# Loading q, k and v six chunks ahead instead of four in a fused attention and MLP kernel

## The chip, the cores and the metric

The kernel runs on one core of a Trainium2 chip. The metric is the device time of one execution in microseconds (us). The time of a kernel is a median over several executions on one chip, with the lowest and highest beside it; a point in time or a wait inside the kernel comes from one profiled execution. TensorE is PE in the profile, VectorE is DVE, ScalarE is ACT, GpSimd is POOL and SyncE is SP.

## The reference

```python
def _attn_ref(q, k, v):                      # q, k, v: 8 x 8 x 576 x 64, float32
    scores = scale * np.matmul(q, k.transpose(0, 1, 3, 2))
    Dmat = np.where(rel >= 0, gamma[:, None, None] ** rel[None], 0.0)   # decay by distance
    return np.matmul(scores * Dmat[None], v)

def _moe_ref(x, w_in, w_out):                # x: 4608 x 512; d_ff 2048
    h = x @ w_in
    g = h * np.clip(h + 3.0, 0.0, 6.0) / 6.0
    return g @ w_out
# reference: the attention's output, 4608 tokens of 512, goes through the MLP
```

## The kernel before

The attention works in chunks of 128 rows of one batch, all eight heads at once, with a running state between chunks. A batch of 576 rows gives four such chunks and one of 64 rows. There are 40 chunks, counted from 0; numbers 4, 9, 14 and so on are the small ones. Each chunk is loaded as float32, cast to half precision on GpSimd, transposed, and multiplied on TensorE. The MLP follows block by block, its matmuls woven between the chunks' work.

The load of a chunk takes a staging buffer and puts DMAs into the queue of SP: three of 256 KB for a full chunk, six of 64 KB for a small one.

```python
def load(b, c):
    t  = work.tile([P, 2, H, D] ..., FP32, tag="stgqk", bufs=5)
    tv = work.tile([P, H, D] ...,    FP32, tag="stgv",  bufs=5)
    for dst, src in ((t[:, 0], k), (t[:, 1], q), (tv, v)):
        if c < NCH:
            nc.sync.dma_start(dst, src[b, :, P*c:P*c + P, :]...)          # L86
            continue
        for x in range(2):
            nc.sync.dma_start(dst[x*REM:x*REM + REM], src[b, ...]...)     # L92
```

Steps carry the number of their chunk; the first after the opening is step 4. The step of chunk i does chunk i's work on TensorE, casts chunk i + 2, sends its transpose into the same queue, and loads a later chunk. The opening has loaded the first ones.

```python
def step(i):
    ...                                   # inter, update, keep, score, mix
    stage(cast, i + 2)                    # GpSimd
    if i + 2 > NCH + NPE - 1:
        stage(xpose, i + 2)               # nc.sync.dma_start_transpose, L124
    stage(load, i + 4)                    # L488
# ... in the opening:
    stage(load, NCH)
    for i in range(NCH + 1, NCH + 4):     # NCH = 4
        stage(load, i)
```

The second matmul of the MLP ends in a copy on ScalarE to a buffer of the pool `osb`, and the output DMA goes into SP's queue as well.

```python
def down(kb, mc, part):
    ...                                   # matmuls into pout, L526
    if part == 3:
        osb = work.tile([P, 2, DM], FP32, tag="osb", bufs=3)
        nc.scalar.copy(osb[:, 0], pout)                                    # L531
        nc.sync.dma_start(out[tok0 + P*mc:tok0 + P*mc + P, :], osb[:, 0])  # L533
```

## Time and profile before

| | kernel before |
|---|---|
| time, median (lowest to highest) of 4 runs | 315.67 us (314.45 to 322.81) |
| span of the profiled run, granted clock | 314.4 us, 0.995 |
| TensorE busy | 296.8 us, 94% |
| ScalarE's wait for an output DMA (fourth copy to `osb`) | 2.00 us, ends at 52.30 us |
| TensorE's waits for transposes near 96 and 102 us | 1.59 + 1.92 us |

How to read it: TensorE is the bound over most of the span, so a change of the loads can only matter in the short stretches in which TensorE stands still, and in what such a stretch does to the clock afterwards. For a DMA queue each timeline row is the start, the time that SP spent issuing, the line, and "out<-in". SP's rows stand in program order, so a row also shows what stood behind what. For an engine, the bracket at the end of a row is the idle time before it and what ended that. The prediction below shows these rows of the kernel before.

### The profile page before, as it was taken

How to read it: one execution, taken by the hardware profiler on the slowest of the kernel's cores; microseconds unless marked ns; L12 is line 12 of the kernel's file. 1: busy time of each engine (PE TensorE's matmuls, PEld its weight loads, DVE VectorE, ACT ScalarE, POOL GpSimd, SP SyncE). 2: the span in 40 equal slices, each digit the busy share in tenths (PEclk: the TensorE clock that was granted, in tenths of full speed). 3: DMA queues.
4: the chain of work that ended last, by engine and by line, in shares of the span. 5: the costliest groups of instructions: out<-in, count | busy, mean ns of one | idle time of the engine just before them, and what ended most of it. 6: DMA issues, size and time to landing. Idle time of an engine off the chain costs nothing.

```text
span 314.4 us, 6863 instructions
## 1 busy us (share of the span) xinstructions
PE 296.8 (94%) x2644; PEld 190.6 (61%) x2644; DVE 233.4 (74%) x435; ACT 162.4 (52%) x307; POOL 127.0 (40%) x154
## 2 busy tenths in 40 slices
PE   7899989989995998999999999999989999999994
PEld 2454447667542467656864686468646865684583
DVE  6797348475766599799778977897779778856781
ACT  7667235446435461476257624753566357526721
POOL 2780167462855479144073607231844070000000
PEclk9999999999999799999999999999999999999999
DMA  7999998739879969965259865980799252003003
GB/s 249 219 207 197 196 224 220 199 90 217 165 177 220 255 143 201 247 150 126 60 144 291 163 144 141 262 185 19 179 255 248 56 178 9 2 0 135 1 0 133
DMA packets 143264, 49.59 MB, mean 158 GB/s; under 512 B 134272, under 2 KB 140416, under 8 KB 143232
## 3 DMA queue, kind: packets, MB, share of 16 engines
q1 hardware_dynamic: 139008, 44.97, 62.0%
q0 software_dynamic: 4224, 4.19, 8.0%
q8 instruction: 20, 0.33, 0.4%
q14 instruction: 12, 0.10, 0.1%
HBM read 36.70 MB, written 9.44 MB: 147 GB/s over the span
## 4 chain that ended last, share of the span: by engine, by line
PE 64%; DMA 18%; POOL 6%; DVE 4%; ACT 3%; issue 2%; SPq 2%; POOLq 0%; DVEq 0%; ACTq 0%
PE ph L509 28%; PE accy L582 14%; DMA wout_160<-in_moe_w_out_dram 7%; PE accz L582 7%; PE pout L526 4%; PE accx L582 3%; DMA stgk_72<-in_k_dram 2%; PE po L354 2%; DMA qkt_4_3592<-natqk_4_3587 2%; ACT u L513 2%; DMA qkt_0_1558<-natqk_0_1553 2%; DMA out_dram<-osb 1%; DMA stgv_0_1791<-in_v_dram 1%; PE pu L274 1%; DMA stgqk_1_1498<-in_k_dram 1%
## 5 line engine op out<-in xcount | busy, mean ns | idle before, releaser
L513 ACT ACTIVATE u<-ph,cb 128x512 f32<-128x512 f32 x144 | 98.8, 689 | 36.0 <-PE ph L509 33.9
L509 PEld LDWEIGHTS <-win_159 128*128 128x128 f16 x704 | 62.1, 98 | 60.2 <-issue 2.8
L592 ACT COPY csum<-accy 128x256 f32<-128x256 f32 x42 | 15.7, 373 | 45.1 <-PE accy L582 45.1
L310 POOL TENSOR_TENSOR sd<-state_152,gp 128x512 f32<-128x512 f16 x7 | 7.3, 1040 | 39.2 <-DVE state_152 L305 26.2
L310 POOL TENSOR_TENSOR sd<-state_153,gp 128x512 f32<-128x512 f16 x7 | 7.3, 1041 | 25.7 <-DVE state_153 L305 16.5
L310 POOL TENSOR_TENSOR sd<-state_151,gp 128x512 f32<-128x512 f16 x7 | 7.3, 1040 | 24.0 <-DVE state_151 L305 16.8
L509 PE MATMUL ph<-xt_1198,win_159 128*128 128x512 f16 x64 | 16.1, 410 | 0.0
L526 PE MATMUL pout<-wout_160,gt_0_505 128*128 128x512 f16 x64 | 15.0, 379 | 0.9 <-DMA wout_160<-in_moe_w_out_dram 0.9
L514 DVE SCALAR_TENSOR_TENSOR gt_4_1565<-u,ph 128x512 f16<-128x512 f32 x16 | 10.7, 685 | 5.6 <-ACT u L513 5.6
L509 PE MATMUL ph<-xt_342,win_159 128*128 128x512 f16 x64 | 14.0, 379 | 0.7 <-ACT xt_342 L387 0.7
L509 PE MATMUL ph<-xt_2035,win_159 128*128 128x512 f16 x64 | 14.5, 380 | 0.0
L509 PE MATMUL ph<-xt_3027,win_159 128*128 128x512 f16 x64 | 14.5, 380 | 0.0
L509 PE MATMUL ph<-xt_3585,win_159 128*128 128x512 f16 x64 | 14.3, 379 | 0.0
L509 PE MATMUL ph<-xt_1617,win_159 128*128 128x512 f16 x64 | 14.3, 379 | 0.0
L509 PE MATMUL ph<-xt_2592,win_159 128*128 128x512 f16 x64 | 14.3, 379 | 0.0
L509 PE MATMUL ph<-xt_4018,win_159 128*128 128x512 f16 x64 | 14.0, 379 | 0.0
L514 DVE SCALAR_TENSOR_TENSOR gt_10_4472<-u,ph 128x512 f16<-128x512 f32 x16 | 11.0, 687 | 3.8 <-ACT u L513 3.8
L601 DVE TENSOR_TENSOR osb<-accz,csum 128x256 f32<-128x256 f32 x14 | 5.9, 423 | 10.5 <-PE accz L582 10.4
L608 DVE TENSOR_TENSOR osb<-accz,csum 128x256 f32<-128x256 f32 x14 | 5.8, 422 | 10.5 <-ACT csum L592 10.5
L514 DVE SCALAR_TENSOR_TENSOR gt_0_505<-u,ph 128x512 f16<-128x512 f32 x16 | 11.0, 687 | 2.6 <-ACT u L513 2.5
L514 DVE SCALAR_TENSOR_TENSOR gt_9_4109<-u,ph 128x512 f16<-128x512 f32 x16 | 10.8, 686 | 2.6 <-ACT u L513 2.4
L514 DVE SCALAR_TENSOR_TENSOR gt_8_3599<-u,ph 128x512 f16<-128x512 f32 x16 | 10.5, 683 | 2.8 <-ACT u L513 2.6
(736 smaller groups left out, 685.9 us busy)
## 6 DMA issues: line engine op xcount, KB each, us to landing
out_dram<-osb SPq DMA_DIRECT2D x14, 512.0 KB, 4.2
win_159<-in_moe_w_in_dram POOLq DMA_DIRECT2D x4, 512.0 KB, 9.5
wout_160<-in_moe_w_out_dram POOLq DMA_DIRECT2D x4, 512.0 KB, 18.3
out_dram<-osb SPq DMA_DIRECT2D x8, 256.0 KB, 3.6
stgq_66<-in_q_dram SPq DMA_DIRECT2D x1, 512.0 KB, 3.8
stgk_68<-in_k_dram SPq DMA_DIRECT2D x1, 512.0 KB, 4.6
stgq_70<-in_q_dram SPq DMA_DIRECT2D x1, 512.0 KB, 6.2
stgk_72<-in_k_dram SPq DMA_DIRECT2D x1, 512.0 KB, 7.0
```

Of the source, the lines that this page charges most:

```text
L274: nc.tensor.matmul(pu[:, pr, :], n16[:, 0, cs], v16[:, cs], start=True, stop=True)
L310: nc.gpsimd.tensor_tensor(out=sd, in0=ss, in1=gch, op=ALU.mult)
L354: nc.tensor.matmul(o_ap, v_ap, a_ap, start=(c == 0 and pr == 0), stop=True, skip_group_check=True)
L509: nc.tensor.matmul(ph[:, j, :], win16[:, dmc, P * fc:P * fc + P], xts[kb][:, dmc, :], start=(dmc == 0), stop=(dmc == NCC - 1))
L513: nc.scalar.activation(u, ph, ACTF.Relu, bias=cb[:, 0:1], scale=1.0 / 6.0)
L514: nc.vector.scalar_tensor_tensor(out=gts[kb][:, g * m:g * m + m, :], in0=u, scalar=1.0, in1=ph, op0=ALU.min, op1=ALU.mult)
L526: nc.tensor.matmul(pout, gts[kb][:, fc, P * mc:P * mc + P], wout16[:, fc, :], start=(fc == 0), stop=(fc == NFC - 1))
L582: nc.tensor.matmul(o, a[:, f, u, :], w[:, f, :], start=(first and f == 0), stop=(f == HF - 1), skip_group_check=True)
L592: nc.scalar.copy(c, o)
L601: nc.vector.tensor_tensor(out=osb[:, 0, HD:DM], in0=o, in1=st["c", u, 6], op=ALU.add)
L608: nc.vector.tensor_tensor(out=osb[:, 1, HD:DM], in0=st["z", u][:, 0:HD], in1=c, op=ALU.add)
```

## The change

The intent: a chunk's data should have landed long before GpSimd casts it, so that casts and transposes never wait for a load. The five staging buffers stay as they are.

```diff
@@ step
         if i + 2 > NCH + NPE - 1:
             stage(xpose, i + 2)
-        stage(load, i + 4)
+        stage(load, i + 6)
@@ opening
     stage(load, NCH)
-    for i in range(NCH + 1, NCH + 4):
+    for i in range(NCH + 1, NCH + 6):
         stage(load, i)
```

## The prediction

> **What bounds the kernel now.** I read the page first, then the chain of work that ended last, then the waits of TensorE, and last the timelines of the DMA queue (SP), ScalarE (ACT) and TensorE (PE) around the places that the chain names.
>
> ```profile
> span 314.4 us, 6863 instructions
> PE 296.8 (94%) x2644; PEld 190.6 (61%) x2644; DVE 233.4 (74%) x435; ACT 162.4 (52%) x307; POOL 127.0 (40%) x154
> PEclk9999999999999799999999999999999999999999
> ```
>
> PE is busy for 94% of the span, so loads can only matter in the stretches where PE waits. Stretch by stretch, from 120 to 278 us PE is busy all but about 1.4 us; the holes lie before 110 us and at 231 us. The waits of PE say how many of them a DMA ended:
>
> ```profile
> PE pm_1678 L323 <- DMA qkt_0_1558<-natqk_0_1553: 1.9, 1, 1.9
> PE pm_1595 L327 <- DMA qkt_4_1496<-natqk_4_1491: 1.6, 1, 1.6
> PE pm_3716 L327 <- DMA qkt_4_3592<-natqk_4_3587: 1.1, 1, 1.1
> PE pout L526 <- DMA wout_160<-in_moe_w_out_dram: 0.9, 1, 0.9
> ```
>
> These are waits for a DMA transpose of an already cast chunk (or for weights), none for a load of q, k or v directly. The first two stand at 96 and 102 us and have a price on top: in the one-microsecond stretches of 103 to 106 us the granted clock is 0.50 (the 7 in the PEclk row). 16 matmuls there take 5.24 us, against 3.63 us in the same row form before, so about 1.7 us more. All that earlier loads could win is thus 1.9 + 1.6 + 1.1 + 1.7 = 6.3 us, 2.0% of 314.4, if every one of these waits went away.
>
> Now the DMA queue, in which everything that SP issues stands in one order: loads, outputs, transposes.
>
> ```profile
> 44.72 0.89 SPq L86 DMA_DIRECT2D stgqk_3_700<-in_k_dram  x1
> 45.65 0.98 SPq L86 DMA_DIRECT2D stgqk_3_700<-in_q_dram  x1
> 46.73 1.02 SPq L86 DMA_DIRECT2D stgv_3_701<-in_v_dram  x1
> 47.84 1.28 SPq L533 DMA_DIRECT2D out_dram<-osb  x2
> 49.21 1.86 SPq L92 DMA_DIRECT2D stgqk_4_785<-in_k_dram  x2
> 51.12 1.27 SPq L92 DMA_DIRECT2D stgqk_4_785<-in_q_dram  x2
> 52.49 1.25 SPq L92 DMA_DIRECT2D stgv_4_786<-in_v_dram  x2
> ...
> 54.96 0.42 SPq L86 DMA_DIRECT2D stgqk_0_950<-in_k_dram  x1
> 55.43 0.72 SPq L86 DMA_DIRECT2D stgqk_0_950<-in_q_dram  x1
> 56.24 1.21 SPq L86 DMA_DIRECT2D stgv_0_951<-in_v_dram  x1
> ```
>
> The queue is back to back from 10 to 57 us: it is late, because the weights of the MLP took the DMA engines until 42 us (one load's issue took 9.65 us at 21.43). The first two outputs go out at 47.84 us only because the queue reached them then; the first had been ready since ScalarE copied it at 43.3 us. And the next lines, of ScalarE, show who was waiting for that:
>
> ```profile
> 43.32 0.59 ACT L531 COPY osb<-pout 128x512 f32<-128x512 f32 x1 [2.42 <-PE pout L526]
> ...
> 52.30 0.59 ACT L531 COPY osb<-pout 128x512 f32<-128x512 f32 x1 [2.00 <-DMA out_dram<-osb]
> 52.78 2.43 ACT L513 ACTIVATE u<-ph,cb 128x512 f32<-128x512 f32 x4
> 55.08 1.04 ACT L222 COPY qkt_1_906<-pst 128x1024 f16<-128x1024 f16 x1
> ```
>
> There are three osb buffers, so the fourth copy waits 2.00 us for the first output to land (47.84 + 4.36 = 52.20 in the chain), with four activations and a copy behind it. PE waits for that last copy: its next matmul, at 56.17 us, notes 0.48 us for qkt_1_906. The chain runs through exactly these pieces. So this output is on the path already, with no slack.
>
> **What the Trainium skill says.** "DMA: Bandwidth & Descriptors", section "Rules for kernel authors", advises issuing a DMA early and waiting late; that is the change's intent. The same page, "Anatomy of one DMA — SWDGE (gpsimd) path", says that DMA engines do not wait on semaphores and that a wait happens on the issuing sequencer before dispatch; so a load ahead of an output holds it up. The trace agrees: the output ready at 43.9 us left at 47.84. "TensorE: Matmul & The Clock Gate", Part 1, gives half clock after an idle window of about 3.4 us; here 0.50 for about 3.4 us followed idle stretches of 1.6 and 1.9 us, so it needs less than a wholly idle window.
>
> **The change, part by part.** No compute instruction is added or removed; the built program's queue has the same DMAs in another order. I read that order, with its waits, against the one before. Chunks are counted from 0, five to a batch; each fifth one (rows 512 to 575) takes six small DMAs, the others three.
>
> *Start.* Six chunks (4 to 9) are loaded in the opening, and chunk 10 in the first step, where before it was four and chunk 8. The queue before: chunk 7, chunk 8, outputs 1 and 2, chunk 9, outputs 3 and 4, chunk 10. After: chunks 7, 8, 9, 10, outputs 1 and 2, chunk 11, outputs 3 and 4, chunk 12. With five staging buffers chunk 9 takes the buffer of chunk 4 (cast by 22.3 us) and chunk 10 that of chunk 5 (cast by 42.5 us), so these loads don't stall at 48 us; they simply stand before output 1. They cost what they cost now: 49.21 to 53.74 = 4.5 us for chunk 9 and 54.96 to 57.45 = 2.5 us for chunk 10, 7.0 us; at the pace of a less loaded stretch (1.27 us a pair, and 0.58 + 0.57 + 0.88) it would be 3.8 + 2.0 = 5.8. I take 6.3 us. Output 1 leaves at about 54.1 and lands near 58.5; the fourth copy starts then, not at 52.30; PE gets its first gt_1 tile, which it now reads at 54.44, near 60.5. A hole of some 6 us opens in PE: **+6.3 us**, since neither PE nor ScalarE had slack there and both run their lists in order.
>
> *Clock.* A hole of that length should bring one half-clock stretch with it, of which part falls in the hole and part on mixed work: **+1.2 us**, an estimate (between 0 and 2.5) from the 1.7 us that the 3.4 us at 103 us cost.
>
> *The hole at 96 to 103 us.* From 83.9 to about 113 us the queue is back to back again, and the transposes wait for its order. The cast of chunk 15 waits 2.05 us for its load now; two chunks earlier, that load has landed. And the six-DMA load of chunk 14 (83.92 to 88.2 us) moves two steps up, away from right before these transposes, with a three-DMA load (2.1 us) in its place. Stepping through: the transpose of chunk 13 can go at 86.8 (its cast ends at 86.7) where it went at 88.32; that of chunk 14 at 91.2 where it was 92.76; that of chunk 15 at 95.6 where it was 97.37. The wait of 1.6 us goes, most of that of 1.9 stays, since PE then arrives sooner: about 1.8 us won, and with a chance of a third the 1.7 us of slow clock: **-2.3 us**.
>
> *The rest.* From 120 us on PE is the bound. The transpose of chunk 34 at 226.28 us stands behind three loads and two 512 KB outputs in both orders, so its 1.1 us stays: 0. A load six ahead needs the buffer of chunk i+1, but the transpose of chunk i+2, before it in the queue, waits for a later cast; so no new buffer wait in the steady state. Bytes are the same.
>
> Sum: 6.3 + 1.2 - 2.3 = +5.2 us on the median of 315.77: 321.0 us.
>
> **The rivals.**
> (a) *Earlier loads win.* GpSimd's waits for loads (2.05 us at 92.88, 3.9 us at 232.9, 1.5 us here and there) vanish, the holes at 96 to 103 close, clock included, and the output is late by less than I think. For it: those waits are in the profile. Against: the bound of 6.3 us, and that the queue's issue time, which stays, makes these transposes late. With 4 us won and a delay of 2, 313.5 us.
> (b) *Nothing moves.* Transfers are hidden for most of the span (PE 94% busy), and the output's delay is taken up: the DMA engines could serve the small loads faster, or the start's loss moves into the queue-bound stretch at 83 to 103 us and is absorbed there. Against: that stretch begins when casts that follow PE's own work are done, so it shifts along. 316 to 318 us.
> (c) *It is worse than summed.* Later outputs are pushed back too, and the clock stays low for two windows: 7.0 + 2.5 - 1.0 = +8.5, 324 us.
>
> **Range and chances.** The delay is the surest part in sign, 5 to 7 us; the clock 0 to 2.5; the gain 1 to 4. Combined, +1 to +9 us: 316.5 to 324.5. Slower by 2% begins at 322.1, a little above my value: 0.33. Faster by 2% would need all of the 6.3 us with no delay: 0.04. Within: 0.63.
>
> **What would show it.** In the queue's timeline of the changed kernel nine load DMAs stand between 47.8 us and the first output, which leaves near 54; ScalarE's fourth osb copy waits 7 to 9 us instead of 2.00 for that output; PE has one hole of about 6 us before 61 us and the PEclk row a dip after it; the waits for qkt_4 and qkt_0 near 100 us (now some 6 us later) shrink from 3.5 us to about 1.7; GpSimd's waits for stgqk near there are gone; from 126 us on the kernel is the old one, shifted. I am wrong if the output leaves before 51 us, if the fourth copy waits under 4 us, or if PE keeps working across that wait.

## The result, and the profile after

| | before | after |
|---|---|---|
| time, median (lowest to highest), 4 runs each | 315.67 us (314.45 to 322.81) | 324.2 us (322.45 to 324.68) |
| ratio, 95% interval | | 1.0273 [1.0217, 1.0329] |
| span, granted clock of the profiled run | 314.4 us, 0.995 | 322.6 us, 0.984 |

A ratio is the mean time of one kernel's runs over the mean of the other's runs of the same rounds, so it is not quite the ratio of the medians. Executions over 1.5% slower than the fastest of the same kernel are left out of the means. The changed kernel is slower, by 2.7%. The predicted 321.0 us is 3.2 us short of the median, which lies just inside the range of 316.5 to 324.5; "within 2%" had been called likelier than "slower".

The page of the kernel after: the busy row and the granted clock in 40 slices.

```profile
span 322.6 us, 6876 instructions
PE 299.8 (93%) x2644; PEld 191.3 (59%) x2644; DVE 233.7 (72%) x435; ACT 162.4 (50%) x307; POOL 125.9 (39%) x154
PEclk9999999789999889999999999999999999999999
```

The work is the same: 2644 matmuls, the same busy ScalarE. There are two dips of the clock now, in the slices of about 56 to 73 us and of about 105 to 121 us; before there was only one. In stretches of one microsecond the first has half clock from about 60 to 66.7 us and the second from about 111 to 114 us.

The SP queue's timeline of the kernel after, around the first output:

```profile
48.50 2.77 SPq L92 DMA_DIRECT2D stgqk<-in_k_dram  x2
51.33 1.27 SPq L92 DMA_DIRECT2D stgqk<-in_q_dram  x2
52.69 1.26 SPq L92 DMA_DIRECT2D stgv<-in_v_dram  x2
54.05 0.56 SPq L86 DMA_DIRECT2D stgqk<-in_k_dram  x1
54.65 0.58 SPq L86 DMA_DIRECT2D stgqk<-in_q_dram  x1
55.33 1.10 SPq L86 DMA_DIRECT2D stgv<-in_v_dram  x1
56.53 1.27 SPq L533 DMA_DIRECT2D out_dram<-osb  x2
```

Six DMAs of chunk 9 and three of chunk 10 stand ahead of the two outputs, which leave at 56.53 us instead of 47.84. The first of them had been ready since ScalarE's first copy at 43.81 us. ScalarE's timeline of the kernel after shows who paid:

```profile
43.81 0.59 ACT L531 COPY osb<-pout 128x512 f32<-128x512 f32 x1 [2.92 <-PE pout L526]
...
60.34 0.59 ACT L531 COPY osb<-pout 128x512 f32<-128x512 f32 x1 [9.54 <-DMA out_dram<-osb]
60.82 2.43 ACT L513 ACTIVATE u<-ph,cb 128x512 f32<-128x512 f32 x4
```

The fourth copy waits 9.54 us, not 2.00, for the first output to land and free its buffer. The activations behind it wait along, and so does TensorE, whose timeline after reads:

```profile
54.48 0.61 PE L220 MATMUL pst<-ident,natqk 128*128 128x128 f16 x8
62.29 1.89 PE L526 MATMUL pout<-wout,gt 128*128 128x512 f16 x4 [7.20 <-DVE gt L514]
...
65.08 2.69 PE L526 MATMUL pout<-wout,gt 128*128 128x512 f16 x8
```

TensorE stands for 7.20 us. The profile names VectorE's tile gt as the releaser, but VectorE only passed on what ScalarE gave it late. After the hole eight matmuls take 2.69 us; the same eight took 1.90 us before. The end of this stretch, the matmuls of line 354 for the next chunk, moved from 58.55 to 67.93 us, by 9.38 us. At the end of the span 8.2 us of that are left.

Were the waits that the change aimed at removed? GpSimd's waits for loads were: after 60 us the trace of before has 18 of them, the longest 2.05 us at 92.88 and 3.88 us at 232.86; the trace of after has none. But what TensorE waits for is the transpose, and its waits after read:

```profile
PE pout L526 <- DVE gt L514: 7.2, 1, 7.2
PE pm L323 <- DMA qkt<-natqk: 2.1, 2, 1.7
PE pm L327 <- DMA qkt<-natqk: 1.8, 2, 1.1
```

(The columns are total us, times, longest.) Against 1.9 + 1.6 + 1.1 us in the same view of before, the two transpose rows still hold 3.9 us.

### The profile page after: what moved, and what is told of

Same layout as the page of the kernel before. It is cut to its first block, busy times and chain, and to the rows that moved or that the text cites. A ratio compares the mean times of both kernels' runs of the same rounds, so it can differ in the third digit from the quotient of the medians.

```text
span 322.6 us, 6876 instructions
## 1 busy us (share of the span) xinstructions
PE 299.8 (93%) x2644; PEld 191.3 (59%) x2644; DVE 233.7 (72%) x435; ACT 162.4 (50%) x307; POOL 125.9 (39%) x154
## 4 chain that ended last, share of the span: by engine, by line
PE 59%; DMA 20%; POOL 7%; DVE 4%; SPq 3%; issue 3%; ACT 2%; POOLq 0%; DVEq 0%; ACTq 0%
PE ph L509 27%; PE accy L582 13%; DMA stgqk<-in_k_dram 7%; DMA qkt<-natqk 7%; PE accz L582 6%; PE accx L582 3%; DMA win<-in_moe_w_in_dram 3%; PE pout L526 2%; POOL natqk L111 2%; PE po L354 2%; DMA stgk<-in_k_dram 2%; PE pm L323 2%; POOL natqk L110 2%; DVE gsum L562 2%; POOL natv L114 2%
## 5 line engine op out<-in xcount | busy, mean ns | idle before, releaser
L509 PE MATMUL ph<-xt,win 128*128 128x512 f16 (+2 forms) x704 | 131.8, 343 | 0.8 <-ACT xt L387 0.7
L514 DVE SCALAR_TENSOR_TENSOR gt<-u,ph 128x512 f16<-128x512 f32 x144 | 96.2, 685 | 42.9 <-ACT u L513 41.7
L509 PEld LDWEIGHTS <-win 128*128 128x128 f16 x704 | 61.9, 98 | 60.6 <-issue 2.4
L582 PEld LDWEIGHTS <-gsum 128*128 128x128 f16 x448 | 43.7, 98 | 6.6 <-DVE gsum L562 1.6
L526 PE MATMUL pout<-wout,gt 128*128 128x512 f16 x128 | 32.3, 395 | 8.6 <-DVE gt L514 7.2
L333 DVE TENSOR_TENSOR at<-pm,cmask 128x512 f16<-128x512 f32 x56 | 36.1, 686 | 1.1 <-PE pm L323 0.3
L582 PEld LDWEIGHTS <-gt 128*128 128x128 f16 x336 | 31.8, 98 | 6.3 <-DVE gt L514 0.4
L111 POOL TENSOR_TENSOR natqk<-stgqk,wvq 128x512 f16<-128x512 f32 x28 | 32.0, 1142 | 5.9 <-DMA stgqk<-in_q_dram 5.8
L114 POOL TENSOR_TENSOR natv<-stgv,wvq 128x512 f16<-128x512 f32 x28 | 31.1, 1112 | 5.2 <-DMA stgv<-in_v_dram 5.2
L582 PE MATMUL accy<-wt,gsum 128*128 128x256 f16 x224 | 26.9, 273 | 1.0 <-DVE gsum L562 1.0
L526 PEld LDWEIGHTS <-gt 128*128 128x128 f16 x128 | 11.6, 100 | 22.0 <-DVE gt L514 7.4
```

Source lines behind the costliest of these rows:

```text
L111: nc.gpsimd.tensor_tensor(out=n16[:, 1], in0=t[:, 1], in1=w[:, 1].unsqueeze(2).to_broadcast(sh), op=ALU.mult)
L114: nc.gpsimd.tensor_tensor(out=v16, in0=tv, in1=w[:, 0].unsqueeze(2).to_broadcast(sh), op=ALU.mult)
L333: nc.vector.tensor_tensor(out=at, in0=pms[e], in1=w[:, e], op=ALU.mult)
L509: nc.tensor.matmul(ph[:, j, :], win16[:, dmc, P * fc:P * fc + P], xts[kb][:, dmc, :], start=(dmc == 0), stop=(dmc == NCC - 1))
L514: nc.vector.scalar_tensor_tensor(out=gts[kb][:, g * m:g * m + m, :], in0=u, scalar=1.0, in1=ph, op0=ALU.min, op1=ALU.mult)
L526: nc.tensor.matmul(pout, gts[kb][:, fc, P * mc:P * mc + P], wout16[:, fc, :], start=(fc == 0), stop=(fc == NFC - 1))
```

## The experiments

Theory A, after the traces: in the one queue of SP the added opening loads hold back the first output; its `osb` buffer comes free late; the fourth copy, ScalarE and TensorE wait for that; the deeper lookahead itself gives back some 2 us later. The rivals, B and C, put the loss elsewhere than in that buffer and that opening. All runs gave correct results and were timed in five rounds. The kernel before was timed in each of the three groups: 317.01 us (314.34 to 318.87) beside the first four runs, 316.73 us (314.57 to 318.4) beside the next four, 316.86 us (314.77 to 318.77) beside the last two, each of 11 runs. It spreads more there than in the first four runs, so differences of about 1 us between ratios are not to be leaned on.

The most direct test, a fourth `osb` buffer, did not build: SBUF had 150.2 KB left per partition and the pool needed 154. So two outputs share a buffer instead, one in each half.

### The changed kernel, outputs sharing buffers

```diff
+    halfs = []
     def down(kb, mc, part): ...
-            osb = work.tile([P, 2, DM], FP32, tag="osb", bufs=3)
-            nc.scalar.copy(osb[:, 0], pout)
+            if not halfs:
+                osb = work.tile([P, 2, DM], FP32, tag="osb", bufs=3)
+                halfs.extend([osb[:, 0], osb[:, 1]])
+            o = halfs.pop(0)
+            nc.scalar.copy(o, pout)
             ...
-            nc.sync.dma_start(out[...], osb[:, 0])
+            nc.sync.dma_start(out[...], o)
```

> The changed kernel with its queue order kept, but two outputs of 128 rows share one osb tile (the second uses the half that lay unused), so that the fourth copy of ScalarE waits for no output. Theory A (outputs behind the two extra loads hold an osb buffer, ScalarE stands in order behind it, PE behind ScalarE): the wait of 9.54 us and PE's hole of 7.2 us vanish, the slow clock at 62 us too, and what is left is the gain at the transposes, 1.7 us, and some 0.5 us of the old wait: about 313.5 us, ratio 0.990 to 0.996. Theory B (the two extra chunks in the opening take DMA bandwidth from the weights and from the first chunks): the loads are the same, so 322 to 324 us stay. Theory C (six ahead in five buffers makes loads wait for casts): likewise 322 to 324 us.

Measured: 316.55 us (315.39 to 317.61), ratio to before 0.9989 [0.9944, 1.0033]. The loss is gone. The SP queue's timeline of this kernel and, below it, ScalarE's timeline:

```profile
57.41 1.02 SPq L86 DMA_DIRECT2D stgv<-in_v_dram  x1
58.52 1.65 SPq L538 DMA_DIRECT2D out_dram<-osb  x2
```

```profile
53.40 0.59 ACT L536 COPY osb<-pout 128x512 f32<-128x512 f32 x1 [0.31 <-PE pout L528]
```

This is the telling pair. The output leaves even later than in the changed kernel, at 58.52 us (this profiled run started some 2 us late, waiting for weights), still behind nine loads. But the fourth copy no longer waits for it, there is no hole in TensorE, and the clock row has no dip. A late output alone cost next to nothing; a late output that holds a needed buffer cost about all of the 2.7%. The step of A about the cause is confirmed, and B and C fall as causes of this loss. But the ratio is above the 0.990 to 0.996 that A expected: the gain from the lookahead is not there.

### The kernel before, outputs sharing buffers

The edit is the one above, applied to the kernel before.

> The kernel before with the same sharing of osb tiles. Theory A: its wait of 2.00 us for the first output goes, but PE only waited 0.5 us of it, so 0.3 to 0.7 us less, ratio 0.997 to 0.999, and the holes near 96 to 103 us stay. This is the base for the first run: under A the first run is 1.5 to 2.5 us faster than this one.

Measured: 314.7 us (314.55 to 315.76), ratio 0.9932 [0.9888, 0.9976]. That is more than expected; a part may be the spread of before on that chip. What matters is the pair: with the buffer wait out of both, six ahead (316.55) should have been 1.5 to 2.5 us faster than four ahead (314.7) if the lookahead gains anything, and it is 1.85 us slower. So a small cost of the depth itself, as C has it, is not excluded; no run isolates one.

### Six ahead, but only from step 6 on

```diff
-        stage(load, i + 4)
+        for d in range(4, 5 if i < 6 else 7):
+            stage(load, i + d)
```

The opening is that of before, so the outputs keep their early place.

> The opening of the kernel before (four chunks, then one a step), and six ahead only from the seventh step on: two chunks more are issued at 57 us, where the queue has nothing to do until 60 us and both outputs before it have gone. Theory A: no loss at 52 us, and the gain near 100 us of about 1.7 us alone: 313.5 us, ratio 0.992 to 0.997. Theory C (six in five buffers costs in the steady state): 316 us or more, as any such cost is still in it.

Measured: 316.13 us (314.98 to 318.1), ratio 0.9982 [0.9936, 1.0028]: no loss and no gain to be seen, where 0.992 to 0.997 was expected. The time also meets C's 316 us or more, but the kernel before ran at 317.01 us beside it, so that figure tells nothing here. TensorE's waits for transposes stay, 1.44 us at 96.01 and 1.63 us at 102.14, about the 1.59 and 1.92 of before.

### The opening of the change alone

```diff
-        stage(load, i + 4)
+        stage(load, i + (6 if i < 7 else 4))
-    for i in range(NCH + 1, NCH + 4):
+    for i in range(NCH + 1, NCH + 6):
```

> The opening of the changed kernel (six chunks, six ahead for the first steps), then no loads for two steps and four ahead as before. Theory A: the whole loss of some 9.4 us and none of the gain: 325 us, ratio 1.028 to 1.034, with ScalarE's wait of about 9.5 us and PE's waits for the transposes of some 3.5 us near 106 to 112 us. Theory C: the steady state is the old one, so the loss should mostly go, below 1.015.

Measured: 322.68 us (320.84 to 323.84), ratio 1.0177 [1.0129, 1.0225]. The fourth copy waits 8.52 us at 59.17 and TensorE 6.2 us for gt. The opening alone makes most of the loss; C's figure, below 1.015, is missed, though the interval reaches below it. The ratio is under the 1.028 to 1.034 that A expected, partly because before ran at 317.0 here, and the trace has no second dip of the clock near 110 us. TensorE's waits for the transposes of chunks 14 and 15 are 1.45 and 1.36 us, less than the 3.5 us expected.

### Five ahead

```diff
-        stage(load, i + 4)
+        stage(load, i + 5)
-    for i in range(NCH + 1, NCH + 4):
+    for i in range(NCH + 1, NCH + 5):
```

> Half the dose: loads five chunks ahead, so that only chunk 9 (six DMAs, 5.5 us in the queue of the changed kernel) stands before the first two outputs, not chunk 10 as well. Theory A (the output behind the loads): the first output leaves at 53 to 54 us, ScalarE's fourth copy waits 6 to 7.5 us, PE's hole is 4 to 5 us, the kernel 315.7 + 5 to 6.5 us, ratio 1.014 to 1.022. If the loss came from any other part of being further ahead, the hole would not scale with the output's place in the queue.

Measured: 320.26 us (319.37 to 321.22), ratio 1.0106 [1.0069, 1.0143], below the expected 1.014 to 1.022, but with the output leaving at 53.87 us as expected. The copy's wait of 5.54 us and TensorE's hole of 3.19 us also fall short of the 6 to 7.5 and 4 to 5 us expected. ScalarE's timeline of this kernel:

```profile
56.30 0.59 ACT L531 COPY osb<-pout 128x512 f32<-128x512 f32 x1 [5.54 <-DMA out_dram<-osb]
```

With none, six and nine added load DMAs ahead of the output the fourth copy waits 2.00, 5.54 and 9.54 us. The wait follows the queue in order, and A's sizes were too large.

### The changed kernel, outputs issued by ScalarE

```diff
-            nc.sync.dma_start(out[...], osb[:, 0])
+            nc.scalar.dma_start(out[...], osb[:, 0])
```

If only the order in SP's queue held the output, another engine's queue should free it.

> The changed kernel with its eight outputs of 128 rows issued from ScalarE's queue, right behind the copies that make them, and nothing else changed: three osb buffers as before. Theory A: the first output no longer stands behind loads, lands before 50 us, and the fourth copy does not wait; PE's hole vanishes although the buffers are as few as they were; ratio 0.992 to 1.002, less what ScalarE spends on issuing. If the hole stayed, the number of buffers or the DMA engines, not the order of the queue, would be the cause.

Measured: 326.11 us (325.12 to 328.5), ratio 1.0296 [1.0252, 1.034]. A clear miss: no better than the change, and not the test of the queue's order alone that was meant. ScalarE's timeline of this kernel shows where the output stood.

```profile
43.47 0.59 ACT L531 COPY osb<-pout 128x512 f32<-128x512 f32 x1 [2.54 <-PE pout L526]
54.13 0.38 ACTq L533 DMA_DIRECT2D out_dram<-osb  x1
54.56 0.45 ACT L387 ACTIVATE xt<-po 128x128 f16<-128x128 f32 x2 [10.50 <-DMA stgv<-in_v_dram]
```

Between its copy at 43.47 us and its DMA at 54.13 us ScalarE waits for a load of v. The built program says why: the DMAs of SP and ScalarE share eight completion semaphores (counters that say when a DMA is done), and each DMA waits before its issue until the one that last had its semaphore has completed. The first output's semaphore was last given to a v load of chunk 9, five DMAs earlier in the program, which still stood deep in SP's queue. So the other queue did not cut the output loose from the loads, and now the wait stops ScalarE's compute as well: TensorE waits 9.91 us for a copy of ScalarE. In the source nothing of this is to be seen.

### Six ahead late, with shared buffers

The third edit and the first together.

> The late start of six ahead together with the shared osb tiles: neither the loss nor the old wait. From the earlier runs the lookahead itself won nothing that shows (transposes waited for as long as before), so this should equal the kernel before with shared osb tiles: ratio 0.991 to 0.996. If lookahead wins after all, 0.985 to 0.990.

Measured: 316.02 us (314.77 to 316.52), ratio 0.997 [0.9931, 1.0009], slightly above the 0.991 to 0.996 expected. The waits for transposes are 0.79, 1.71 and 1.13 us at 92.07, 97.09 and 102.73. Six ahead without any loss at the start still gains nothing over four ahead with shared buffers (ratio 0.9932).

### Using the depth to clear the queue

The loads of steps 11, 12 and 31 are held back behind the transposes that TensorE waits for; being up to six ahead makes that possible without starving GpSimd. From step 11 on the edit also lets the depth fall to four, and to five from step 20 to 31, so that the head start is used up and not made good; the holds and this smaller depth were not tested apart.

```diff
-        for d in range(4, 5 if i < 6 else 7):
-            stage(load, i + d)
+        far = 4 if i < 6 else 6 if i < 11 else 4 if i < 20 else 5 if i < 32 else 4
+        for d in range(4, far + 1):
+            if i not in (11, 12, 31):
+                stage(load, i + d)
```

> The same, but the head start is spent: in the eleventh, twelfth and thirty-first step no load is issued, so that the transposes of chunks 14, 15 and 34, for which PE waits, stand in the queue without a load before them; the loads follow later. Theory D (these transposes are late because of what is in the queue and on the DMA engines ahead of them, and a lookahead that keeps the same number of loads between them changes nothing): PE's waits near 96 and 102 us (1.4 and 1.6 us in the late-six run) fall below 0.5 us each, that at 231 us (1.1 to 1.4) too, so 2.5 to 4 us less than the run before this one: ratio 0.980 to 0.988. If the casts or the transposes themselves are what is slow, nothing changes against the run before this one.

Measured: 311.7 us (310.79 to 312.45), ratio 0.9834 [0.9798, 0.987], as expected, 4.3 us faster than the run before it and faster than both kernels. The SP queue's timeline of this kernel:

```profile
87.77 1.79 SPq L124 DMA_TRANSPOSE qkt<-natqk  x1
89.66 0.52 SPq L541 DMA_DIRECT2D out_dram<-osb  x1
90.28 1.22 SPq L124 DMA_TRANSPOSE qkt<-natqk  x1
91.59 0.53 SPq L541 DMA_DIRECT2D out_dram<-osb  x1
92.22 1.31 SPq L124 DMA_TRANSPOSE qkt<-natqk  x1
```

The transposes of chunks 13, 14 and 15 start 2.51 and 1.94 us apart, where in the kernel before they were 4.44 and 4.61 us apart with three loads between each pair. TensorE's waits for transposes in this kernel:

```profile
PE pm L323 <- DMA qkt<-natqk: 2.0, 3, 0.9
```

The waits for the transposes of chunks 14, 15 and 34 are gone from this view; 0.92 us at 92.02 and 0.84 us at 165.55 are the longest left.

### Four ahead, with the same idea

The second kernel (four ahead, shared buffers) with the loads of steps 12 and 31 held back by one step. Step 11 cannot be held as well at this depth, since its chunk is cast two steps later.

```diff
-        stage(load, i + 4)
+        if i not in (12, 31):
+            stage(load, i + 3)
+            stage(load, i + 4)
```

> The kernel before with shared halves (four chunks ahead), holding the loads of steps 12 and 31 back by one step, behind the transposes of chunks 14/15 and 34. It asks whether the gain of the held version (0.9834) needs the depth. Theory H (the gain is from an empty queue ahead of the transposes, the depth only makes the holding possible): most of the two waits that the hold of step 12 can touch (the one for chunk 15, 1.6 us or so, and 1.1 us at 231) goes, but chunk 16 is loaded only just before its cast, and at four ahead step 11 can't be held, so ratio 0.986 to 0.993, slower than the six-ahead held version. Theory D (the depth itself matters, holding without it only moves the wait to GpSimd's cast of chunk 16): ratio 0.993 or above, with a new wait of 2 us or more of GpSimd for stgqk and PE waiting for chunk 16's transpose.

Measured: 314.01 us (312.68 to 317.46), ratio 0.9904 [0.9856, 0.9951]. This lies in H's range, and the wait for chunk 15's transpose is gone; that for chunk 14's stays, 1.74 us at 95.95, and 1.27 us for that of chunk 35 come up at 234.57. The sign of theory D of this text came too: GpSimd waits 4.58 us at 100.28 for the load of chunk 16 and 4.27 us at 227.63 for that of chunk 35, but only the second reaches TensorE. The interval overlaps that of four ahead without a hold, so H is favoured and not proved. That the depth helps by allowing the second hold is what the two held kernels suggest.

### Twice the DMAs for the same bytes

Why did transposes not come earlier with six ahead? My guess by then was that the moved load has twice the bytes. The test splits the three loads of chunk 16, ahead of the transpose of chunk 13, into six; the rest is the kernel of "six ahead late, with shared buffers".

```diff
+            if (b, c) == (3, 1):
+                for x in range(2):
+                    nc.sync.dma_start(dst[64*x:64*x + 64], src[b, ...]...)
+                continue
             if c < NCH:
```

> The late six-ahead kernel with shared halves (ratio 0.997), with one thing changed: the three 256 KB loads of chunk 16, which stand before the transpose of chunk 13, are issued as six DMAs of 128 KB. Same bytes, twice the issues. Theory bytes (this stretch of the queue is held by the data that the DMA engines have to move): the transpose of chunk 13 starts later by under 0.7 us, and the one of chunk 15 by under 0.5 us; time within 0.5 us of 316.0, ratio 0.995 to 0.999. Theory issue (the count of DMAs sets the pace, as my prediction stepped it): the six take about 3.9 us in the queue instead of 2.1, both transposes start 1.5 us or more later, PE's waits for them grow by about as much, ratio 1.000 to 1.004.

Measured: 317.12 us (315.13 to 319.58), ratio 1.0009 [0.9958, 1.0061]. The transpose of chunk 13 starts at 89.40 us, not 87.67: 1.73 us later, as the theory of the issue count has it. That of chunk 15 starts at 99.48 instead of 98.30: 1.18 us later, so part of the push is taken up on the way, and neither theory holds as written. TensorE's waits for the transposes of chunks 13 to 15 grow from 3.63 to 4.78 us in all. The count of issues sets when the first transpose goes; something else stretches the two after it. The time of the whole run does not separate the theories.

## Why the prediction was right or wrong

**The output behind the loads: right in mechanism, short in size.** Nine load DMAs stand ahead of the first output, ScalarE's fourth copy waits for it and TensorE has one hole. Predicted was +6.3 us; the fourth copy came 8.04 us later (52.30 to 60.34). The sentence of the skill that the prediction leans on speaks of waits on the issuing sequencer; here the nine loads stand back to back in the queue, and it is the 8.03 us of their issue that held the output. The queue before the loads was already 0.66 us late (48.41 us against 47.75). The term that was mis-sized is the load of chunk 9: I took 3.8 to 4.5 us for it, and it held the queue 5.55 us (48.50 to 54.05), because its first pair of issues took 2.77 us. Chunk 10 took the 2.5 us predicted (54.05 to 56.53). The changed kernel with shared buffers shows that this buffer is the cause: the output stays late and the loss goes. The opening-only run and the five-ahead run show that it is the opening.

**The clock: right in size, in part by luck.** Predicted +1.2 us for one half-clock stretch like the one at 103 us, which lasted some 3.4 us. This one lasted some 6.8 us, from about 59.9 to 66.7, but 2.4 us of that fell into the hole. The stretch moved by 9.38 us by line 354, where the copy had moved by 8.04: the difference of about 1.3 us includes the eight matmuls that took 2.69 us instead of 1.90; the rest was not taken apart. (The prediction's 1.7 us for 103 us is a little large: 5.24 - 3.63 is 1.61 us.)

**The gain at 96 to 103 us: the step that failed.** I predicted -2.3 us. In the profiled run the matmul behind chunk 15's transpose moved from 102.53 to 110.25, by 7.72 us, so 1.66 us of the 9.38 came back there. But this is no gain of lookahead: wherever the start was made equal, six ahead was no faster than four. The opening-only kernel, four ahead by then, points the same way: its line 354 came 7.52 us late (66.07 against 58.55) and its matmul behind chunk 15's transpose 6.31 us late (108.84 against 102.53), so 1.21 us came back without the depth. Most of the 1.66 us thus looks like a late start that is absorbed. The span from the fifth `osb` copy to the end, where the start is out of the account, shows no gain either ("late six" is the kernel that is six ahead only from step 6 on):

| kernel | loads ahead after the start | fifth copy to end, us |
|---|---|---|
| before | 4 | 314.4 - 60.02 = 254.4 |
| before, shared buffers | 4 | 314.0 - 60.26 = 253.7 |
| opening only | 4 | 319.6 - 67.54 = 252.1 |
| after | 6 | 322.6 - 69.39 = 253.2 |
| after, shared buffers | 6 | 315.9 - 62.43 = 253.5 |
| late six | 6 | 313.0 - 60.58 = 252.4 |
| late six, shared buffers | 6 | 313.1 - 60.36 = 252.7 |
| late six, shared buffers, chunk 16 split | 6 | 316.1 - 60.61 = 255.5 |
| five ahead | 5 | 318.4 - 66.17 = 252.2 |
| four ahead with holds, shared buffers | 4 | 312.3 - 59.65 = 252.7 |
| held loads, shared buffers | up to 6 | 309.6 - 60.08 = 249.5 |

These are single traces. Four ahead without holds spans 252.1 to 254.4 and six ahead without the split 252.4 to 253.5; only the version with three holds stands apart as faster.

The wrong sentence is "Stepping through: the transpose of chunk 13 can go at 86.8 ...; that of chunk 15 at 95.6 where it was 97.37". I kept the distances between the transposes as they were and moved only the first. Between the transposes of chunks 13 and 15 the queue has the same instructions at both depths: two transposes, six loads of 256 KB and two outputs. These are the three transposes in the SP queue's timeline before, then in that of late six with shared buffers:

```profile
88.32 1.27 SPq L124 DMA_TRANSPOSE qkt_3_1427<-natqk_3_1422  x1
...
92.76 1.30 SPq L124 DMA_TRANSPOSE qkt_4_1496<-natqk_4_1491  x1
...
97.37 1.47 SPq L124 DMA_TRANSPOSE qkt_0_1558<-natqk_0_1553  x1
```

```profile
87.67 2.19 SPq L124 DMA_TRANSPOSE qkt<-natqk  x1
...
93.44 1.25 SPq L124 DMA_TRANSPOSE qkt<-natqk  x1
...
98.30 1.30 SPq L124 DMA_TRANSPOSE qkt<-natqk  x1
```

From the first to the last they took

| kernel | transpose of 13 to that of 15, us |
|---|---|
| before | 88.32 to 97.37: 9.05 |
| before, shared buffers | 88.35 to 97.80: 9.45 |
| opening only | 94.86 to 104.11: 9.25 |
| after | 95.33 to 105.99: 10.66 |
| after, shared buffers | 90.58 to 101.19: 10.61 |
| late six | 86.91 to 97.95: 11.04 |
| late six, shared buffers | 87.67 to 98.30: 10.63 |
| the same, chunk 16 split | 89.40 to 99.48: 10.08 |

So the transpose of chunk 13 does go earlier (86.91 and 87.67 us with late six, 88.32 and 88.35 with the plain start and four ahead), as stepped, and that of chunk 15 does not (97.95 and 98.30 against 97.37 and 97.80). The windows of the two traces show what differs around it; first before, then after (columns: stretch, us, busy us and count of PE, PEld, DVE, ACT, POOL, then clock, share of the DMA engines busy, GB/s):

```profile
84.00:90.00 6.00, 6.00 (x56) 3.22 (x55) 2.46 (x5) 1.58 (x3) 4.71 (x7) 1.00 0.47 107
90.00:98.00 8.00, 5.98 (x54) 3.03 (x53) 4.68 (x9) 3.74 (x7) 3.89 (x5) 1.00 1.00 237
```

```profile
91.00:97.00 6.00, 6.00 (x56) 3.24 (x55) 3.33 (x7) 1.18 (x2) 4.81 (x6) 1.00 1.25 227
97.00:106.00 9.00, 8.33 (x74) 4.30 (x73) 5.95 (x12) 4.18 (x7) 7.64 (x10) 1.00 1.04 243
```

Ahead of the first of these transposes the six small loads of before leave the DMA engines half idle (0.47, 107 GB/s); the full-size load that six ahead puts in their place has them full (1.25, 227 GB/s). After that both move some 240 GB/s. That the issues take longer because more bytes are still outstanding is my reading of the windows: it fits the shorter 10.08 us where the split gave the engines time, but no run isolates it, and it stays open.

**The rest: right.** From 126 us on the kernel is the old one shifted: the wait for chunk 34's transpose is 1.12 us at 240.32, where it was 1.1 us at 231.

**The sum.** 6.3 + 1.2 - 2.3 = 5.2 was predicted; measured by chunk 15 are 8.04 + 1.34 - 1.66 = 7.72 us, and the spans differ by 8.2 us, so some 0.5 us came after it.

**The rivals.** (a) was right that GpSimd's waits for loads vanish and wrong that time follows, since TensorE waits for transposes that stand in the queue. (b) fell with the 9.54 us wait, but its absorption in the stretch of 83 to 103 us is there in small, as the opening-only kernel shows. (c) came nearest, at 324, with causes close to its own: a larger delay, and half clock for 6.8 us, twice as long as at 103 us before. Of the signs named in advance, those of the start came true in kind, each beyond its figure: the output left at 56.53 us (near 54), the copy waited 9.54 us (7 to 9), the hole was 7.20 us and ended at 62.29 (about 6, before 61). The one for the transposes near 100 us half did (2.37 us left, about 1.7 expected).

## What to carry to other kernels

Before loading deeper, list what else goes through the same in-order queue, and find each store whose buffer somebody needs soon: the store's place in the queue is then part of the compute path. A wait that disappears on an engine off the path, here all 18 waits of GpSimd for loads, is no gain until the thing the bound engine waits for comes earlier. Depth paid here only in the kernel that spent it on holding loads back at the moments when short, urgent DMAs had to pass.

## What the Trainium skill lacked or had wrong

- "DMA: Bandwidth & Descriptors", section "Rules for kernel authors", says to issue a DMA early and wait late. It doesn't add that an early load delays whatever is issued behind it: nine loads moved an output from 47.84 to 56.53 us and the kernel got 2.7% slower.
- The same page, section "Issuing engines are not separate DMA queues", says that issuing from several engines saves only time on the sequencer. Here it did harm: with completion semaphores shared between the two engines' DMAs, ScalarE stood 10.50 us around an output's issue, waiting for a load of SP's queue. No page that I read speaks of a wait across queues that comes from reusing a completion semaphore.
- "TensorE: Matmul & The Clock Gate", Part 1, ties half clock to an idle window of about 3.4 us; for shorter gaps it gives no length. The trace of before has clock 0.50 near 103 us after idle stretches of 1.59 and 1.92 us with matmuls between them; four ahead with holds has one from about 97 to 100 us after a single stretch of 1.74 us, and four ahead with shared buffers, with 1.75 and 1.64 us, has none there. Shorter gaps can be enough, and which ones was not settled.
- None that I read has the cost of issue on a busy queue: a pair of 64 KB loads took 1.27 us of SP's time in most places of the kernel after and 2.77 us at 48.50, and that was the main error in my largest term.
